# Joint image-text attention block on one core: image V in 512-column tiles with a shared 128-column remainder, and text scores, image gate rows and text V moved behind all image scores

## The chip, the cores and the metric

The kernel runs on one core of a Trainium2 chip, in one launch. The metric is device time in microseconds, the median of several executions. The core has a matrix engine (TensorE, PE in the profile), a vector engine (VectorE, DVE), a scalar engine (ScalarE, ACT), a general engine (GpSimd, POOL) and a queue engine that only issues transfers (SyncE, SP). Each engine works through its own instruction list in order; they meet at semaphores.

## The reference

Two batches. Each has 256 image tokens and 32 text tokens of width D = 1152; everything is bfloat16. Fourteen matrices of 1152 x 1152 (2.65 MB each) are read, each once.

```python
mod_i = silu(c) @ wmod_img          # first three of six slices used: shift, scale, gate
mod_t = silu(c) @ wmod_txt
hi = layernorm(x_img) * (1 + sci) + shi
ht = layernorm(x_txt) * (1 + sct) + sht
qi, ki, vi = split(hi @ wqkv_img);  qt, kt, vt = split(ht @ wqkv_txt)
q, k, v = concat([qt, qi]), concat([kt, ki]), concat([vt, vi])
p = softmax(q @ k.T * D ** -0.5)
at, ai = split(p @ v)
out_i = x_img + gai * (ai @ wo_img)
out_t = x_txt + gat * (at @ wo_txt)
```

## The kernel before

A D of 1152 is nine blocks of 128 (`KT`), so every product over D is a run of nine matrix instructions that add up in one PSUM tile. PSUM has eight tiles in two pools: six of `ps_mm` and two of `ps_tr`; a tile is taken in turn, and a new user waits until the reader of the old one is done.

**Loads.** SP issues all weight loads into five slots of one matrix each, in a fixed order: `x_i` for batch 0 (L103), the image scale `w_sc_i` in four pieces (L107), then image V `w_v_i` in five pieces (L109) with the two tiles of `x_i` of batch 1 between them (L112), then image shift, image Q, text shift, text x, image K, text scale, text Q, text K, image gate, text V, the two output matrices and the text gate. A load waits for the last use of its slot's former content; the last piece of `w_v_i` has four of the nine blocks.

**Image stage** (to the first Q instruction). LayerNorm: image tiles 0 and 2 get their sums on ACT (`ln_sums`, L199 and L200), tiles 1 and 3 theirs on DVE (`ln_stats`, L192); ACT works out the reciprocal deviations (L209, L210), DVE normalises (L214) into `xn`. PE transposes `xn` (`x_transposes`, six 128x128 transposes to a PSUM tile `tp`, copied to `xT_i` by ACT or DVE at L250). The scale rows come from `sc_rows`, matrix instructions that use 32 columns of the array (four side by side), and DVE turns them to columns (`sc_cols`, L257) and multiplies `xT_i` into `hS_i` (`x_scale`, L264). V needs only the scaled input; what the shift adds to V is a row that is added later. `v_open` runs image V in accumulators of 384 columns: six (`V0`) for batch 0 over eight of the nine blocks, then the transposes of batch 1, the ninth block, then the six of batch 1 (`V1`), with the shift rows `mod_rows_of(w_sh_i)` between. The layer norm of batch 1 stands in the ACT and DVE lists behind the scaling of batch 0:

```python
sc_cols(5, KT)
x_scale(4, KT, 0)
s2 = ln_sums(x_i[:, 2, :], xn_b[1][:, 0, :])
...
v_open(V0, 0, K8)
out01, out31 = x_transposes(0, 1), x_transposes(3, 1)
```

Then `hT_i`, with the shift, is made in place of `xT_i` (L346, L349), and `shift_v_rows` works out the row that V lacks.

**Q and K** (`qk_img`, 81 instructions of 512 columns each, then `qk_txt`) run without a gap on PE; DVE sums the text shift beside them (`shift_part`, L427).

**Attention.** Scores are nine instructions for each of four image query tiles (`scores_img`) and one text tile (`scores_txt`, 32 columns of the array). `soft_max`, `soft_exp` and `soft_div` are the DVE maximum (L556), the ACT exponential (L563), and the division on DVE (L568, L570), in which POOL writes a second copy of the last 32 columns (L571). `img_gate` runs the image gate rows on PE (32 columns), ACT copies them out (L508), and POOL writes them to a scratch tensor with two DMAs (L510), from which `img_gate_spread` later reads them back for all partitions (L521). `p_transposes` turns the probabilities for the second product, and ACT copies them (L606); `v_txt` is text V, 64 columns of the array, two side by side. The order on PE is: two image scores, text scores, gate rows, two image scores, nine transposes, text V, nine transposes, then `attn_pair`, then `out_img` and `out_txt`. `keep_in_program_order` (`pin`) holds all PE instructions, and the marked ones of the other engines, in the order of the source.

Of the kernel before, what the change touches and what calls it, by code (L numbers as in the profile page):

```python
# [14 lines left out]
def kernel(  # L15
# [14 lines left out]
    nc = tc.nc  # L30
    bf = mybir.dt.bfloat16
    f32 = mybir.dt.float32
# [27 lines left out]
    def mm(*a, **k):  # L60
        return pin(nc.tensor.matmul(*a, **k))  # L61

    def tr(*a, **k):
        return pin(nc.tensor.transpose(*a, **k))  # L64
# [38 lines left out]
    nc.sync.dma_start(x_i[:, 0:TPB, :], x_img[0].rearrange("(p t) d -> p t d", t=TPB))  # L103
# [4 lines left out]
    for r0, r1 in ((0, 1), (1, 2), (2, 3), (3, 5), (5, KT)):  # L108
        nc.sync.dma_start(w_v_i[:, r0:r1, :], v_v[:, r0:r1, :])  # L109
        if r0 in (1, 3):  # L110
            i = TPB + r0 // 2
            nc.sync.dma_start(x_i[:, i, :], x_img[1].rearrange("(p t) d -> t p d", t=TPB)[i - TPB])  # L112
# [67 lines left out]
    def evac(out_ap, in_ap):  # L180
        if evac_idx[0] % 2 == 0:
            nc.vector.tensor_copy(out_ap, in_ap)
        else:
            nc.scalar.copy(out_ap, in_ap)
        evac_idx[0] += 1
# [21 lines left out]
    def ln_rstd(var, np_, sign=1.0):  # L207
        rstd = small.tile([P, 1], f32, tag="rstd")
        pin(nc.scalar.activation(rstd[0:np_, :], var, ACT.Ln, bias=eps_t[0:np_], scale=sign))  # L209
        pin(nc.scalar.activation(rstd[0:np_, :], rstd[0:np_, :], ACT.Exp, scale=-0.5))  # L210
        return rstd

    def ln_norm(x_ap, mean, rstd, np_, out_ap):
        pin(nc.vector.tensor_scalar(out_ap, x_ap, mean, rstd[0:np_, :], op0=ALU.subtract, op1=ALU.mult))  # L214

    xn_b = [act.tile([P, TPB, D], bf, tag="A%d" % b, name="xn%d" % b) for b in range(B)]
# [13 lines left out]
    sc_ps = ps_tr.tile([P, KT, LW], f32, tag="tr")  # L230
# [11 lines left out]
    def x_transposes(k0, b):  # L242
        tp = (ps_tr if b else ps_mm).tile([P, 3, NI], bf, tag="tr" if b else "mm", name="tp")
        for kt in range(k0, k0 + 3):
            for t in range(TPB):
                tr(tp[:, kt - k0, t * P:(t + 1) * P], xn_b[b][:, t, kt * P:(kt + 1) * P], ident[:])
        dst = xT_i[:, k0:k0 + 3, b * NI:(b + 1) * NI]

        def copy_out():
            pin(nc.vector.tensor_copy(dst, tp[:]) if k0 == 3 else nc.scalar.copy(dst, tp[:]))  # L250

        return copy_out
# [14 lines left out]
    v_b = [act.tile([P, TPB, D], bf, tag="A%d" % b, name="v%d" % b) for b in range(B)]  # L267
    accs = {}

    def v_open(ids, k0, k1, engines=None):  # L270
        for key in ids:
            if key not in accs:
                accs[key] = ps_mm.tile([P, CH], f32, tag="mm", name="vps")
        for kt, (i, cc) in [(kt, key) for kt in range(k0, k1) for key in ids]:
            mm(accs[(i, cc)][:], lhsT=hS_i[:, kt, i * P:(i + 1) * P], rhs=w_v_i[:, kt, cc * CH:(cc + 1) * CH],
               start=(kt == 0), stop=(kt == KT - 1), skip_group_check=True)
            if kt == KT - 1:
                dst = v_b[i // TPB][:, i % TPB, cc * CH:(cc + 1) * CH]
                if engines:
                    pin((nc.scalar.copy if engines[ids.index((i, cc))] == "A" else nc.vector.tensor_copy)(  # L280
                        dst, accs[(i, cc)][:]))
                else:
                    evac(dst, accs[(i, cc)][:])

    V0, V1 = [[(i, cc) for i in range(b * TPB, (b + 1) * TPB) for cc in range(NCH)] for b in range(B)]

    def ln_norm_dve(i, mv):
        ln_norm(x_i[:, i, :], mv[:, 0:1], ln_rstd(mv[:, 1:2], P), P, xn_b[i // TPB][:, i % TPB, :])

    def ln_norm_act(i, sm):  # L290
        ln_norm(x_i[:, i, :], sm[:, 0:1], ln_rstd(sm[:, 2:3], P, sign=-1.0), P, xn_b[i // TPB][:, i % TPB, :])

    s0 = ln_sums(x_i[:, 0, :], xn_b[0][:, 0, :])
# [3 lines left out]
    ln_norm_act(0, s0)  # L297
    for out in [x_transposes(k0, 0) for k0 in (0, 3, 6)]:
        out()
    sc_rows(0, 4)  # L300
    sc_rows(4, 7)
    warm_up(1)
    sc_rows(7, K8)
    warm_up(1)
    sc_rows(K8, KT)
    sc_cols(0, 1)
    x_scale(0, 1, 0, step=1)
    sc_cols(1, 5)
    x_scale(1, 4, 0)
    sc_cols(5, KT)  # L310
    x_scale(4, KT, 0)
    s2 = ln_sums(x_i[:, 2, :], xn_b[1][:, 0, :])
    ln_var(s2)
    m3 = ln_stats(x_i[:, 3, :], P)
    r2, r3 = ln_rstd(s2[:, 2:3], P, sign=-1.0), ln_rstd(m3[:, 1:2], P)
    ln_norm(x_i[:, 2, :], s2[:, 0:1], r2, P, xn_b[1][:, 0, :])
    ln_norm(x_i[:, 3, :], m3[:, 0:1], r3, P, xn_b[1][:, 1, :])
    v_open(V0, 0, K8)
    out01, out31 = x_transposes(0, 1), x_transposes(3, 1)
    out01()  # L320
    out31()
    x_scale(0, 6, 1)
    v_open(V0[0:2], K8, KT, engines="AA")
    x_transposes(6, 1)()
    v_open(V0[2:], K8, KT, engines="VAVA")
    x_scale(6, KT, 1)
    v_open(V1[0:2], 0, KT)
# [9 lines left out]
    v_open(V1[2:3], 0, KT)  # L337
# [12 lines left out]
    for key in V1[3:]:  # L350
        v_open([key], 0, KT)
# [130 lines left out]
    def v_txt(r):  # L482
        ps = ps_mm.tile([P, VC], f32, tag="mm")
        for kt in range(KT):
            for g in range(2):
                c0 = g * HD + r * VC
                mm(ps[64 * g:64 * g + NTT, :], lhsT=hT_t[:, kt, :], rhs=w_v_t[:, kt, c0:c0 + VC],
                   start=(kt == 0), stop=(kt == KT - 1), tile_position=(0, 64 * g))
        return ps
# [11 lines left out]
    def mod_rows(w_blk, si):  # L501
        gps = ps_mm.tile([P, VC], f32, tag="mm")
        for kt in range(KT):
            for g in range(NGG):
                mm(gps[32 * g:32 * g + 32, :], lhsT=sT32[:, kt, :], rhs=w_blk[:, kt, g * VC:(g + 1) * VC],
                   start=(kt == 0), stop=(kt == KT - 1), tile_position=(0, 32 * g))
        g_sb = work.tile([P, VC], bf, tag="garow")
        pin(nc.scalar.copy(g_sb[:], gps[:]))  # L508
        for b in range(B):
            nc.gpsimd.dma_start(gsc[si, b, :].rearrange("(g j) -> g j", g=NGG), g_sb[b:P:32, :])  # L510
# [5 lines left out]
    def img_gate():  # L516
        mod_rows(w_ga_i, 0)
# [8 lines left out]
    def txt_gate():  # L526
        mod_rows(w_ga_t, 1)
        for g in range(2):
            for b in range(B):
                r0 = 64 * g + 32 * b  # L530
                nc.gpsimd.dma_start(gbf[r0:r0 + NT, :, :],
                                    gsc[1, b, :].rearrange("(r g j) -> g r j", r=2, g=2)[g].partition_broadcast(NT))

    shift_v_rows()
# [59 lines left out]
    def p_transposes(b):  # L594
        pT = work.tile([P, 3, NTOK], bf, tag="pT")
        tiles = [(range(3), ps_tr)] if b == 0 else [((2,), ps_mm), (range(2), ps_tr)]
        for kjs, pool in tiles:
            pT_ps = pool.tile([P, 8 * P], bf, tag="tr" if pool is ps_tr else "mm", name="pT_ps")
            txt = [(2, pbs["t"], ident2 if b else ident)]
            img = [(qi, pbs[(b, qi)], ident) for qi in range(TPB)]  # L600
            for n, kj in enumerate(kjs):
                for qi, pb, perm in (txt + img if b else img + txt):
                    o = n * NTOK + qpos[b][qi]
                    k0 = kj * P - (NT * b if kj == 2 else 0)
                    tr(pT_ps[:, o:o + P], pb[:, k0:k0 + P], perm[:])
            pin(nc.scalar.copy(pT[:, kjs[0]:kjs[-1] + 1, :],  # L606
                               pT_ps[:, 0:len(kjs) * NTOK].rearrange("p (k n) -> p k n", n=NTOK)))
        pTs[b] = pT

    def attn_keys(tiles, first):  # L610
        for b, dt in tiles:
            for kj in range(2):
                mm(tiles[(b, dt)][:], lhsT=v_b[b][:, kj, dt * P:(dt + 1) * P], rhs=pTs[b][:, kj, :],
                   start=(first and kj == 0), stop=(not first and kj == 1))
# [25 lines left out]
    sp = {key: scores_img(*key) for key in I[:2]}  # L640
# [5 lines left out]
    st = scores_txt()  # L646
    half = work.tile([NTT, NTOK], f32, tag="half", bufs=1)
    pin(nc.scalar.copy(half[:], st[NTT:P, :]))
    soft_div(I[1])
    img_gate()  # L650
    pin(nc.vector.tensor_add(half[:], st[0:NTT, :], half[:]))
    soft_max("t", half, NTT)
    soft_exp("t")
    for key in I[2:]:
        sp[key] = scores_img(*key)
    soft_max(I[2], sp[I[2]], P)
    soft_exp(I[2])
    soft_div("t")
    soft_max(I[3], sp[I[3]], P)
    soft_exp(I[3])  # L660
    soft_div(I[2])
    soft_div(I[3])
    p_transposes(0)
    for r in range(2):
        v_txt_out(r, v_txt(r))
    p_transposes(1)
# [76 lines left out]
```

## Time and profile before

| What | us |
|---|---|
| median of three executions (120.5, 121.08, 120.5) | 120.5 |
| the profiled execution: time / span of its trace | 120.5 / 118.6 |
| PE busy | 110.5 (93%) |
| DVE busy / ACT busy / POOL busy | 71.1 / 46.1 / 12.3 |
| mean DMA rate over the span | 346 GB/s |
| first image V instruction | 12.67 |
| first image Q instruction | 37.04 |
| first score instruction | 78.52 |
| first `attn_pair` instruction | 88.29 |
| last PE instruction group starts / span ends | 114.91 / 118.6 |

The span reaches from the first to the last instruction in the trace; the time has 1.9 us more around it. The granted TensorE clock is 0.999 over the span. In a profile line, `out<-in` are tile names, `x18` the number of instructions in a group, and a bracket the idle time of the engine just before, with what ended it.

### The profile page before, as it was taken

The numbers are of one execution on the slowest core, as the hardware profiler recorded it, in microseconds if no ns is written. First come the engines' busy times: TensorE is split into PE (matmuls) and PEld (weight loads), VectorE is DVE, ScalarE is ACT, GpSimd is POOL, SyncE is SP. The second block draws the span as 40 slices with busy tenths as digits, with TensorE's granted clock in tenths as the row PEclk, the third lists the DMA queues.
The fourth block names the chain that finished last, engine by engine and source line by source line (L and its number), as shares of the span: only waits on it lengthen the run. The fifth ranks groups of instructions, "written<-read, shape, count | busy, mean of one in ns | idle before, by whom it ended". The sixth has DMA issues, their size and how long they took to land.

```text
span 118.6 us, 2503 instructions
## 1 busy us (share of the span) xinstructions
PE 110.5 (93%) x1035; PEld 64.7 (55%) x1035; DVE 71.1 (60%) x151; ACT 46.1 (39%) x96; POOL 12.3 (10%) x34
## 2 busy tenths in 40 slices
PE   5999791999999999999999999999999999999990
PEld 1346450655655444444445448687876656566660
DVE  3561863084593999999999030016756656346571
ACT  4765451091292358952521233326557700100000
POOL 7300000000000000000000000002617000470000
PEclk9999999999999999999999999999999999999999
DMA  4999999999999999999999999999999999224223
GB/s 124 368 393 401 409 407 408 413 411 411 410 404 386 319 405 410 416 402 413 390 375 412 412 412 413 405 410 406 411 404 411 417 379 363 100 73 83 100 50 100
DMA packets 19045, 41.02 MB, mean 346 GB/s; under 512 B 1195, under 2 KB 1851, under 8 KB 19035
## 3 DMA queue, kind: packets, MB, share of 16 engines
q1 hardware_dynamic: 18160, 39.86, 87.4%
q0 software_dynamic: 480, 0.89, 2.6%
q10 hardware_dynamic: 395, 0.12, 0.4%
q8 instruction: 8, 0.13, 0.4%
q14 instruction: 2, 0.02, 0.0%
HBM read 39.52 MB, written 1.34 MB: 345 GB/s over the span
## 4 chain that ended last, share of the span: by engine, by line
PE 79%; DMA 15%; SPq 1%; DVE 1%; ACT 1%; issue 0%
PE ps L61 52%; PE vps L61 11%; DMA t<-in_wqkv_img_dram 8%; DMA t<-in_wmod_img_dram 7%; PE gps L61 5%; PE aps L61 5%; PE sps L61 4%; PE pT_ps L64 1%; SPq L107 1%; PE tp L64 1%; ACT xT_i L250 1%; DVE tmp L684 1%; DVE o L685 0%; SPq L103 0%; PE tpt L64 0%
## 5 line engine op out<-in xcount | busy, mean ns | idle before, releaser
L61 PE MATMUL ps<-xT_i,t 128*128 128x512 bf16 x162 | 35.7, 379 | 0.0
L61 PEld LDWEIGHTS <-t 128*128 128x128 bf16 x324 | 20.5, 98 | 18.9 <-issue 0.5
L427 DVE SCALAR_TENSOR_TENSOR acc_sh<-t,sTf,acc_sh 128x1152 f32<-128x1152 bf16 x16 | 21.4, 1408 | 0.0
L61 PE MATMUL vps<-t,hS_i 128*128 128x384 bf16 x108 | 18.4, 326 | 3.2 <-DMA t<-in_wqkv_img_dram 2.6
L61 PE MATMUL ps<-t,aT 128*128 128x384 bf16 (+3 forms) x153 | 20.3, 308 | 0.0
L61 PEld LDWEIGHTS <-aT 128*128 128x128 bf16 (+1 forms) x153 | 12.9, 101 | 7.2 <-issue 0.8
L61 PEld LDWEIGHTS <-hS_i 128*128 128x128 bf16 x108 | 10.3, 98 | 10.3 <-issue 3.0
L357 ACT CAST qkT<-ps 128x512 bf16<-128x512 f32 (+2 forms) x11 | 6.1, 551 | 14.8 <-PE ps L61 13.5
L684 DVE TENSOR_TENSOR tmp<-ps,gb 128x384 bf16<-128x384 f32 (+2 forms) x13 | 6.8, 526 | 8.0 <-PE ps L61 8.0
L571 POOL TENSOR_SCALAR pb<-e,rs 128x32 bf16<-128x32 f32 (+1 forms) x5 | 2.1, 413 | 76.9 <-DVE rs L568 76.9
L355 ACT ACTIVATE qkT<-ps 128x512 bf16<-128x512 f32 (+2 forms) x11 | 6.1, 561 | 8.7 <-PE ps L61 8.7
L61 PE MATMUL wps<-warm 128*128 128x512 bf16 x24 | 7.9, 479 | 1.5 <-DVE unit L129 1.5
L556 DVE TENSOR_REDUCE nmx<-sps 128x1 f32<-128x288 f32 x4 | 1.8, 458 | 9.7 <-PE sps L61 9.7
L61 PEld LDWEIGHTS <-sT 128*32 128x32 bf16 x180 | 4.6, 96 | 2.1 <-issue 1.5
L250 ACT COPY xT_i<-tp 128x768 bf16<-128x768 bf16 x4 | 3.1, 808 | 6.5 <-PE tp L64 6.5
L61 PE MATMUL sps<-qkT 128*128 128x288 bf16 (+1 forms) x54 | 5.5, 287 | 0.0
L620 DVE TENSOR_SCALAR aT<-aps,svc 128x288 bf16<-128x288 f32 x9 | 4.1, 512 | 2.2 <-PE aps L61 2.2
L61 PEld LDWEIGHTS <-warm 128*128 128x128 bf16 x24 | 2.6, 115 | 5.2 <-issue 2.4
L61 PE MATMUL gps<-t,sT 128*32 128x288 bf16 x144 | 5.2, 287 | 0.0
L61 PE MATMUL aps<-pT,v 128*128 128x288 bf16 x36 | 5.1, 287 | 0.0
L61 PE MATMUL ps<-hT_t,t 128*128 128x64 bf16 x162 | 5.1, 193 | 0.0
L622 ACT ACTIVATE aT<-aps,svc 128x288 bf16<-128x288 f32 x9 | 4.3, 500 | 1.4 <-PE aps L61 1.4
(112 smaller groups left out, 104.3 us busy)
## 6 DMA issues: line engine op xcount, KB each, us to landing
t<-in_wqkv_txt_dram SPq DMA_DIRECT2D x3, 2592.0 KB, 16.4
t<-in_wmod_img_dram SPq DMA_DIRECT2D x2, 2592.0 KB
t<-in_wmod_txt_dram SPq DMA_DIRECT2D x2, 2592.0 KB, 16.6
t<-in_wqkv_img_dram SPq DMA_DIRECT2D x3, 864.0 KB, 14.3
t<-in_wqkv_img_dram SPq DMA_DIRECT2D x1, 2592.0 KB
t<-in_wo_img_dram SPq DMA_DIRECT2D x3, 864.0 KB, 8.1
t<-in_wmod_txt_dram SPq DMA_DIRECT2D x2, 864.0 KB, 13.1
t<-in_wo_txt_dram SPq DMA_DIRECT2D x1, 1440.0 KB
```

The lines of the kernel that those rows point to most:

```text
L61: return pin(nc.tensor.matmul(*a, **k))
L64: return pin(nc.tensor.transpose(*a, **k))
L107: nc.sync.dma_start(w_sc_i[:, r0:r1, :], sc_v[:, r0:r1, :])
L250: pin(nc.vector.tensor_copy(dst, tp[:]) if k0 == 3 else nc.scalar.copy(dst, tp[:]))
L355: nc.scalar.mul(out_ap, in_ap, SCALE)
L357: nc.scalar.copy(out_ap, in_ap)
L427: pin(nc.vector.scalar_tensor_tensor(acc, w_sh_t[:, kt, :], col, acc, op0=ALU.mult, op1=ALU.add))
L556: pin(nc.vector.reduce_max(nmx[0:qn, :], sps[0:qn, :], axis=AX.X, negate=True))
L571: pin(nc.gpsimd.tensor_scalar(pb[0:qn, NI + 2 * NT:NI + 3 * NT], e[0:qn, NI:NTOK], rs[0:qn, :], 0.0, op0=ALU.mult, op1=ALU.add))
L620: nc.vector.tensor_scalar(dst, tiles[(b, dt)][:], bias, None, op0=ALU.add)
L622: nc.scalar.activation(dst, tiles[(b, dt)][:], ACT.Identity, bias=bias)
L684: nc.vector.tensor_mul(tmp[:, 0:n], ps[:, 0:n], gb[:, b, c0:c0 + n])
```

## The change

In the image stage it loads all of `x_i` first, and cuts `w_v_i` into six pieces, the last two of two blocks each. It moves the layer norm of batch 1 ahead of the scale rows, and its transposes between them. V runs in tiles of 512 columns: `A0` are four for batch 0, `A1` the first of each tile of batch 1; the second of those follow, and then `v_last`, one PSUM tile with the last 128 columns of all four image tiles. In the attention it puts text scores, gate rows and the first half of text V behind the four image scores; text V runs in 32 columns of the array, four side by side (72 instructions for 36). The copy of the gate rows (`gate_row`) and their two DMAs come after the exponential of the text scores and before `soft_div("t")`. The 18 transposes of the probabilities are adjacent, in four groups, two of which DVE copies.

```diff
-    nc.sync.dma_start(x_i[:, 0:TPB, :], x_img[0]...)
+    for b in range(B):
+        nc.sync.dma_start(x_i[:, b * TPB:(b + 1) * TPB, :], x_img[b]...)
...
-    for r0, r1 in ((0, 1), (1, 2), (2, 3), (3, 5), (5, KT)):
+    for r0, r1 in ((0, 1), (1, 2), (2, 3), (3, 5), (5, 7), (7, KT)):
         nc.sync.dma_start(w_v_i[:, r0:r1, :], v_v[:, r0:r1, :])
-        if r0 in (1, 3):
-            ...
...
+    VW = 512
+    A0 = [(0, 0), (0, 1), (1, 0), (1, 1)]
+    A1 = [(2, 0), (3, 0)]
...
     ln_norm_act(0, s0)
+    s2 = ln_sums(x_i[:, 2, :], xn_i[:, 2, :])
+    m3 = ln_stats(x_i[:, 3, :], P)
+    ln_var(s2)
+    r3, r2 = ln_rstd(m3[:, 1:2], P), ln_rstd(s2[:, 2:3], P, sign=-1.0)
+    ln_norm(x_i[:, 3, :], m3[:, 0:1], r3, P, xn_i[:, 3, :])
+    ln_norm(x_i[:, 2, :], s2[:, 0:1], r2, P, xn_i[:, 2, :])
     for out in [x_transposes(k0, 0) for k0 in (0, 3, 6)]:
         out()
     sc_rows(0, 4)
+    warm_up(3)
     sc_rows(4, 7)
-    warm_up(1)
+    out01 = x_transposes(0, 1)
+    out31 = x_transposes(3, 1)
     sc_rows(7, K8)
-    warm_up(1)
     sc_rows(K8, KT)
+    out61 = x_transposes(6, 1)
+    out01()
     sc_cols(0, 1)
     x_scale(0, 1, 0, step=1)
     sc_cols(1, 5)
-    ...
+    x_scale(1, 3, 0)
+    v_open(A0, 0, 3)
+    out31()
+    out61()
+    x_scale(0, 3, 1)
     sc_cols(5, KT)
-    ...
+    for k0 in (3, 6):
+        for b in range(B):
+            x_scale(k0, k0 + 3, b)
+    v_open(A1, 0, 3)
+    v_open(A0 + A1, 3, KT - 2)
+    v_open(A0 + A1, KT - 2, KT, kt_major=False)
...
+    v_open([(2, 1)], 0, KT)
     p_sh = mod_rows_of(w_sh_i, sT32)
...
+    v_open([(3, 1)], 0, KT)
+    def v_last():
+        vps = ps_mm.tile([P, NIT, P], f32, tag="mm")
+        for i in range(NIT):
+            for kt in range(KT):
+                mm(vps[:, i, :], lhsT=hS_i[:, kt, i * P:(i + 1) * P], rhs=w_v_i[:, kt, 2 * VW:D], ...)
+        evac(v_i[:, :, 2 * VW:D], vps[:])
...
             for g in range(2):
-                mm(ps[64 * g:64 * g + NTT, :], lhsT=hT_t[:, kt, :], ..., tile_position=(0, 64 * g))
+                for b in range(B):
+                    c0, r0 = g * HD + r * VC, 64 * g + NT * b
+                    mm(ps[r0:r0 + NT, :], lhsT=hT_t[:, kt, NT * b:NT * b + NT], ..., tile_position=(0, r0))
...
-    sp = {key: scores_img(*key) for key in I[:2]}
+    sp = {key: scores_img(*key) for key in I}
+    st = scores_txt()
+    img_gate()
+    vt = [v_txt(0)]
...
     soft_exp("t")
...
+    gate_row()
     soft_div("t")
...
+    v_txt_out(0, vt[0])
+    vt.append(v_txt(1))
+    p_transposes(0, (0, 1), ps_tr, nc.scalar.copy)
+    v_txt_out(1, vt[1])
+    p_transposes(0, (2,), ps_mm, nc.vector.tensor_copy)
+    p_transposes(1, (2,), ps_mm, nc.vector.tensor_copy)
+    p_transposes(1, (0, 1), ps_tr, nc.scalar.copy)
```

## The prediction

> **What bounds the kernel now.** First the chain that ended last, since PE is busy 93% of the span and shares alone do not say where a microsecond is worth anything. Columns: start, length, what.
>
> ```profile
> 10.48 9.75 DMA t<-in_wqkv_img_dram
> 20.23 0.04 issue
> 20.27 3.09 PE vps L61 x18
> ...
> 35.82 1.22 PE gps L61 x36
> 37.04 19.53 PE ps L61 x90
> ...
> 78.52 2.92 PE sps L61 x36
> 81.44 1.10 PE gps L61 x36
> 82.55 2.31 PE sps L61 x18
> 84.86 0.50 PE pT_ps L64 x9
> 85.36 2.33 PE ps L61 x36
> 87.69 0.61 PE pT_ps L64 x9
> 88.29 5.78 PE aps L61 x54
> ```
>
> The reader sees a transfer up to 20.23, then PE alone, without a hole, to 114.91. So from the first Q instruction (37.04) on, only fewer PE cycles or a new hole can move the end; before 20.23 it is the arrival of `w_v_i`. The timeline of PE shows the hole, that of ACT what batch 1 waits for:
>
> ```profile
> 12.67 5.05 PE L61 MATMUL vps<-t,hS_i 128*128 128x384 bf16 x30 [0.69 <-DVE hS_i L264]
> 20.27 3.09 PE L61 MATMUL vps<-t,hS_i 128*128 128x384 bf16 x18 [2.56 <-DMA t<-in_wqkv_img_dram]
> ```
>
> ```profile
> 13.37 1.17 ACT L199 ACTIVATE xn<-x_i 128x1152 bf16<-128x1152 bf16 x1 [2.74 <-DMA x_i<-in_x_img_dram]
> ```
>
> Image V begins at 12.67, uses five blocks of weights, and starves for 2.56 us until the one piece with the last four has landed. It has nothing else to do, because batch 1 is not normalised and transposed yet: its `x_i` comes at 13.37, behind other loads.
>
> **Front, step 1: when V can start.** Loads come in issue order at the page's rate, 0.36 to 0.41 MB per us. Running totals from the rate row: 1.18 MB (all of `x_i`) at 5.2 us, with `w_sc_i` 3.83 MB at 11.9, with `w_v_i` 6.49 MB at 18.4. In before, the issue that waits for the last piece of `w_sc_i` ran at 11.19, where the total (3.24 MB) is at 10.4: a piece is usable 0.75 us behind its total. So `x_i` of batch 1 is there at 5.9 and the last scale piece at 12.6 (before: 11.2). ACT is free at 7.8. The two sums of tile 2 take 2.55 us (in before 13.37 to 15.92): 10.35. Variance, two reciprocal deviations and two norms at the spacings of before (L209 to L214) end at 11.9. ACT then copies two of the three `xT_i` tiles of batch 0, which now stand behind these sums, 0.8 us each: 11.15 to 12.65; DVE copies the third, to 12.4. PE's first two transpose groups of batch 1 wait for those two buffers and for norm 2: 12.0 to 12.45 and 12.5 to 12.9. Behind them in PE's list stand the last scale rows, 12.9 to 13.4. From the end of scale rows to V took 0.64 us in before (12.03 to 12.67). **V starts at 14.05, 1.38 us later**; `out61`'s transposes (13.4 to 13.8, after a copy on ACT) fit before that.
>
> **Front, step 2: what V then takes.** The 81 Q instructions of 512 columns with nine others took 19.53 us: 217 ns each. 72 of them: 15.62 us. `v_last` has 36 of 128 columns; the nearest row is the 128x128 transposes, same shape of both operands, 9 in 0.50 us, 55.6 ns: 2.00 us. Two row runs at 1.22: 2.44. In all 20.06 us, if PE never waits. DVE: it scales 128x256 in about 0.22 us; by its list block 0 is ready at 14.05, block 2 at 14.9, batch 1's first three at 16.05, block 3 at 17.05 and 17.7, all at 19; PE wants them at 14.05, 15.8, 16.6, 17.9, 23.1. Weights: blocks 5 and 6 at about 18.5 against 20.5, the last two by 20.2 against 23.1; the hole closes. `w_sh_i`: total at 24.9, plus at most 1.7, against 27.7. `w_q_i`: its last piece is shown by the SP timeline, where the load that waits for it goes out:
>
> ```profile
> 33.06 0.37 SPq L89 DMA_DIRECT2D t<-in_wqkv_img_dram  x1
> ```
>
> **Q starts at 14.05 + 20.06 = 34.11 instead of 37.04: 2.93 us earlier**, 1.05 us after its weights. Where the gain comes from, as a cross-check: 2.56 (hole) + 0.23 (wait for a transpose copy, L250) + about 1.3 (18 transposes taken out of the V run) + 0.3 (columns in fewer instructions), less 1.38.
>
> The Trainium skill, "TensorE: Matmul & The Clock Gate", section Back-to-back issue gap, gives about 81 ns for each 128-column matmul in a stream with its weight load, and that speaks against `v_last`. By it the 36 would take 2.9 us and the whole sum be 0.9 us worse, an estimate from that page; the row says 55.6 ns, and I take the row.
>
> **Middle.** Nothing is edited, so the 2.93 us stay if no load is late. Totals at the page's rate plus 1.7 us (what `w_q_i`'s 33.06 stands behind its total, 31.34), against the moment of need 2.93 us earlier: image K 47.3 against 51.7; text Q 60.3 against 68.7; text K 67.4 against 73; image gate 73.9 against 80.7; text V 80.4 against 81.9; image output 86.9 against 91.6; text gate 93.4 against 97.5. The slack of Q and text V, 1 and 1.5 us, is what the range must hold. DVE's shift sum waits 4.44 us for PE at its end (L447), so it is no bound.
>
> **Tail, PE cycles.** With 0 the first score instruction: four image scores at 1.10, end 4.41; text 0.75 (2.92 less 2.2), 5.16; gate 1.13, 6.29; text V 72 instructions, priced by the gate's 36 in 1.10 as 30.6 ns: 2.20 (before 36 in 2.33), 8.5; 18 transposes about 1.05. That would be 9.55 for 9.77, through fewer changes of array shape.
>
> **Tail, the new wait.** The transposes of key block 2 need the last-32-column copy that POOL writes for text, and POOL's list now has the two scratch DMAs ahead of it. In before POOL did this:
>
> ```profile
> 83.30 1.33 POOL L510 DMA_DIRECT2D mod_scratch<-g_sb  x2 [0.70 <-ACT g_sb L508]
> 84.67 0.30 POOL L571 TENSOR_SCALAR pb<-e,rs 64x32 bf16<-64x32 f32 x1
> ```
>
> There they followed a gate copy at 82.60, one ACT step ahead of the text exponential. Now, with the durations of these rows: `half` on ACT 5.2 to 5.6, image exponential 3 to 6.1, add and maximum on DVE 5.65 to 6.6, text exponential 6.7 to 7.35, gate copy 7.25 to 7.65, POOL's two DMAs 7.95 to 9.28, its copy 9.32 to 9.62. PE arrives after six transposes and two image ones at 9.0, waits to 9.68, then ten transposes: **attention at 10.24 instead of 9.77, 0.47 us later**. Everything on PE stands behind that wait. The ACT and DVE copies of the groups end at 9.7, 10.2 and 10.9, each before its reader. The gate spread begins about 2.5 us later (POOL's wait for the scratch write), lands at about 20 against the first output tile at 17.5; DVE waits, but PE has six buffers, each 1.46 us, and DVE needs 0.92 per chunk, so that is caught up and costs nothing.
>
> The Trainium skill, "SBUF — State Buffer", section Who interferes with whom, says that while VectorE holds the port it shares with GpSimd, GpSimd cannot write the descriptors of its DMAs (about 620 ns alone, 3100 beside such a copy). Two issues at that would add about 5 us to the wait, an estimate from that page, and undo the gain. The row shows 1.33 us for two beside DVE work at 82.84 to 84.35; I take the row.
>
> **Sum.** 120.5 - 2.93 + 0.47 = **118.0 us**, made against the profiled execution, whose time equals the median, 120.5. What can be told from no change is about 0.5%, 0.6 us.
>
> **Rivals.**
> - *Loads take back part (0.20).* Q's or text V's last piece comes 1 to 1.5 us later than reckoned, or V starts later by as much since a step of the ACT chain slips. For it: slacks of 1.05 and 1.5 us, loads at the rate limit throughout. Against: the bytes ahead of both are the same as before. Time 119.0.
> - *No wait in the tail (0.09).* POOL's DMAs start earlier than 7.95 or take no 1.33 us, and attention begins at 9.55: 120.5 - 2.93 - 0.2 = 117.4.
> - *Slower: `x_i` of batch 1 lands late (0.08).* Its ACT sums now stand ahead of batch 0's copies and its transposes ahead of the last scale rows, so if it lands not at 5.9 but with the second scale piece at 11.2, everything up to V moves 3.4 us (11.2 for 7.8): V at 17.45, time 118.0 + 3.4 = 121.4. It decides from a landing at 10.3 (no change). For it: `x_i` of tile 2 came at 13.37 although issued at 4.46. Against: that was behind 3.8 MB of loads; here only 0.59 MB is ahead.
> - *Nothing to be seen (0.08).* V at 16.5 by a slip of half that size, or DMA issues on POOL at twice their price (1.3) together with 1 us lost to loads: 119.9 to 121.1.
>
> **How the numbers follow.** The main case, 0.55, is 118.0. Faster by over 0.5%: 0.55 + 0.20 + 0.09 = 0.84; same 0.08; slower 0.08. The range starts at the case without a tail wait and V 0.2 us early (117.2), and ends at the loads case with 0.5 more, or `v_last` at 81 ns on top of 0.6 lost (119.5).
>
> **What would show it.** Right: first V instruction near 14, no wait of `vps` for a DMA, Q at about 34.1, scores at about 75.6, and a wait of PE for POOL's `pb` before attention at about 85.8. Wrong: a DMA wait at the first Q or text V instruction; V not before 15.5; transposes of batch 1 held by ACT past 13; or an attention that begins under 9.6 us behind the first score.

## The result, and the profile after

The changed kernel takes 118.8 us, the median of six executions (118.58 to 119.04), against a forecast of 118.0 with a range of 117.2 to 119.5. Its ratio to the kernel before is 0.9853, with a 95% interval of 0.9821 to 0.9884; the means behind it are 118.81 and 120.59 us, a fall of 1.8 us. The span of the profiled execution fell as much, from 118.6 to 116.8 us. The ratios here and below leave out executions that took over 1.5% longer than the fastest of their kernel, and with them most, not all, of those in which the granted TensorE clock fell; what that fall is comes with the experiment that fills the hole.

The chain that ended last (start, length, what) no longer has the transfer of image V in it. From 14.36 it is PE up to the text scores:

```profile
14.36 13.77 PE vps L61 x63
28.13 1.22 PE gps L61 x36
29.35 4.06 PE vps L61 x45
33.41 1.22 PE gps L61 x36
34.62 19.53 PE ps L61 x90
...
76.29 5.15 PE sps L61 x54
```

The first Q instruction is at 34.62 (37.04 before), the first score at 76.29 (78.52). In the timeline of PE the hole in V is gone, and there is a short wait for the second scale piece instead:

```profile
11.92 0.55 PE L61 MATMUL sc_ps<-t,sT 128*32 128x288 bf16 x12 [0.39 <-DMA t<-in_wmod_img_dram]
...
14.36 13.77 PE L61 MATMUL vps<-t,hS_i 128*128 128x512 bf16 x63
```

The timeline of ACT shows the sums of batch 1's first tile starting right behind batch 0's work, without the 2.74 us wait for its load that stood there before:

```profile
8.03 1.15 ACT L197 ACTIVATE xn_i<-x_i 128x1152 bf16<-128x1152 bf16 x1
```

The load that waits for `w_q_i` goes out when it did before, so Q now starts 1.5 us behind its weights instead of 4.0 (timeline of SP):

```profile
33.11 0.37 SPq L89 DMA_DIRECT2D t<-in_wqkv_img_dram  x1
```

Then comes the new wait. The chain leaves PE behind the text scores, goes through their softmax, the gate copy on ACT and the two DMA issues on POOL, and comes back to PE at the transposes:

```profile
83.54 0.29 ACT g_sb L520
83.83 0.29 issue
84.12 0.73 POOL mod_scratch L522
84.84 0.00 issue
84.85 0.60 POOL mod_scratch L522
85.44 0.04 issue
85.48 0.31 POOL pb L587
85.79 0.04 issue
85.83 0.73 PE pT_ps L64 x10
86.57 5.78 PE aps L61 x54
```

Attention begins 86.57 - 76.29 = 10.28 us behind the first score, 0.51 us more than the 9.77 of before. From there on nothing moved: from the start of attention to the last `out_img` group it is 26.61 us, against 26.62.

### The profile page after: what moved, and what is told of

It is laid out like the page before. It is cut to its first block, busy times and chain, and to the rows that moved or that the text cites. A ratio compares the mean times of both kernels' runs of the same rounds, so it can differ in the third digit from the quotient of the medians.

```text
span 116.8 us, 2569 instructions
## 1 busy us (share of the span) xinstructions
PE 110.6 (95%) x1072; PEld 63.3 (54%) x1072; DVE 72.3 (62%) x153; ACT 44.1 (38%) x92; POOL 12.3 (11%) x34
## 4 chain that ended last, share of the span: by engine, by line
PE 82%; DMA 8%; DVE 2%; POOL 1%; ACT 1%; SPq 1%; issue 1%; DVEq 0%
PE ps L61 51%; PE vps L61 15%; DMA t<-in_wmod_img_dram 8%; PE aps L61 5%; PE sps L61 4%; PE gps L61 4%; POOL mod_scratch L522 1%; PE sc_ps L61 1%; SPq L104 1%; PE tp L64 1%; PE pT_ps L64 1%; DVE tmp L701 1%; ACT e L579 1%; DVE o L702 0%; DVE half L671 0%
## 5 line engine op out<-in xcount | busy, mean ns | idle before, releaser
L61 PE MATMUL vps<-t,hS_i 128*128 128x512 bf16 (+1 forms) x108 | 17.9, 326 | 0.1
L61 PEld LDWEIGHTS <-hS_i 128*128 128x128 bf16 x108 | 9.0, 98 | 8.7 <-DVE hS_i L264 0.4
L180 DVE CAST v_i<-vps 128x512 bf16<-128x512 f32 x5 | 3.5, 692 | 7.5 <-PE vps L61 7.5
L182 ACT CAST v_i<-vps 128x512 bf16<-128x512 f32 x4 | 2.3, 580 | 9.9 <-PE vps L61 9.9
L61 PE MATMUL aps<-pT,v_i 128*128 128x288 bf16 x36 | 5.1, 287 | 0.0
```

## The experiments

**The image stage alone.** The tail is put back as it was, on the changed image stage.

```diff
-    sp = {key: scores_img(*key) for key in I}
-    st = scores_txt()
-    img_gate()
-    vt = [v_txt(0)]
+    sp = {key: scores_img(*key) for key in I[:2]}
     ...
```

> The changed image stage with the old order of scores, gate, text V and transposes. Theory (all gain is in front, the tail costs about 0.5 us through the wait for GpSimd): first score instruction at about 76.3 as in the changed kernel, 9.77 us from there to attention as in the kernel before, time about 0.5 us below the changed kernel, 118.2 to 118.3. Rival (the tail's fewer changes of array shape are a part of the gain): 0.2 us or more above the changed kernel.

It took 118.55 us, ratio 0.9834 (0.9814 to 0.9854), with spans of 116.1 to 116.4 against 116.6 to 116.8 of the changed kernel. In the chain the first score is at 76.32 and attention at 86.09, which is the 9.77 us of before. The gain is all in front, and the tail gives a part of it back: by the trace 0.51 us, by the spans some 0.45, by the medians, which were not taken side by side, only 0.25.

**The tail alone.** The old image stage with the new tail, that is, the attention part of the change put into the kernel before.

> The old image stage with the new order of scores, gate, text V and transposes. Theory: first score instruction at 78.5 as before, attention 10.25 us behind it with a PE wait of about 0.6 us for GpSimd's copy, time 0.5 us above the kernel before. Rival (fewer changes of array shape win): 0.2 us below the kernel before.

The ratio is 1.0063 (1.0015 to 1.0111), slower. Two of the executions in it had a clock of 0.986; the six of its twelve in which the clock held take 121.10 us on average, against 120.69 for those of the kernel before, 0.4 us more. In its chain the first score stands at 80.86 and attention at 91.14: 10.28 us again, with a PE wait of 0.56 us for POOL. The rival, that fewer changes of array shape win, falls. The profile is of an execution in which the clock fell, and its first score is 2.3 us later than in the kernel before, for a reason told where the hole is filled.

**The gate row late.** Only the order of two lines.

```diff
-    gate_row()
     soft_div("t")
+    gate_row()
```

> The changed kernel with the gate row's copy and its two GpSimd DMAs behind the division of the text scores, so that GpSimd's copy of the last columns comes first. Theory: no wait of PE for GpSimd, attention 9.7 us behind the first score instead of 10.28, time 0.55 us below the changed kernel; the gate spread comes later by about 0.4 us and costs nothing. Rival (the transposes are held by something just behind that wait, the text exponential or the ACT copies): less than 0.2 us gained.

Measured: 118.39 us, ratio 0.9832 (0.9803 to 0.986), and 118.38 beside 118.87 for the changed kernel when both were run together a second time (below). PE waits for POOL no more. What is late next is a short wait for ACT's first copy, in the chain:

```profile
84.75 0.45 PE pT_ps L64 x6
85.20 0.02 issue
85.22 0.65 ACT pT L621
85.87 0.04 issue
85.92 5.94 PE aps L61 x54
```

The chain gives an instruction that waited its own start (85.92 here), and one that did not wait the end of the work before it (86.57 for attention in the changed kernel), so the two can't be set against each other. The timeline of PE gives the own starts of both, first in the changed kernel, then here:

```profile
76.12 5.29 PE L61 MATMUL sps<-qkT 128*128 128x288 bf16 x54
...
86.40 0.90 PE L61 MATMUL aps<-pT,v_i 128*128 128x288 bf16 x6
```

```profile
76.15 5.29 PE L61 MATMUL sps<-qkT 128*128 128x288 bf16 x54
...
85.92 0.90 PE L61 MATMUL aps<-pT,v_i 128*128 128x288 bf16 x6
```

Attention begins 10.28 us behind the first score in the changed kernel and 9.77 us here, as in the kernel before (88.13 - 78.35 = 9.78). So two DMA issues of 1.33 us, moved ahead of a copy of 0.3 us that PE needs, cost the changed kernel 0.51 us, and the times of the two kernels run together differ by as much, 0.49. The 0.2 us that the new order was to save on PE do not show yet, because of the wait for ACT.

**The cut of the last V load, alone, in the kernel before.**

```diff
-    for r0, r1 in ((0, 1), (1, 2), (2, 3), (3, 5), (5, KT)):
+    for r0, r1 in ((0, 1), (1, 2), (2, 3), (3, 5), (5, 7), (7, KT)):
```

> The kernel before with one edit: the last piece of image V (four blocks) is cut into two of two blocks. Theory (the hole at 17.7 to 20.27 is there because the layer norm of batch 1 is late and PE has nothing else): blocks 5 and 6 land near 18.5, PE waits 0.8 us there and then works on; the hole falls from 2.56 to about 1.0 and the time by 1.5 us. Rival (pieces in flight share the rate, so the first half comes hardly earlier): blocks 5 and 6 near 19.8, gain 0.5 us or less. A gain of 1.5 us would mean that over half of the front's gain needs neither the 512-column tiles nor the early layer norm.

119.59 us, ratio 0.993 (0.9908 to 0.9951). The timeline of PE gives the hole:

```profile
18.79 3.09 PE L61 MATMUL vps<-t,hS_i 128*128 128x384 bf16 x18 [1.09 <-DMA t<-in_wqkv_img_dram]
```

It fell from 2.56 to 1.09 us; blocks 5 and 6 are there at 18.75, and the first score comes at 77.20 instead of 78.52. So 1.3 of the 2.2 us in front can be had with one edit of a tuple, without 512-column tiles and without the early layer norm. The time fell by less: 0.8 us by the ratio, 1.0 by the spans (117.7 to 118.0, against a mean of 118.8 for the kernel before). In the profile the other 0.4 us went at the very end, where the waits for the output transfers took 1.5 us in all instead of 1.1; the reason stays open.

**The same load uncut, in the changed kernel.**

```diff
-    for r0, r1 in ((0, 1), (1, 2), (2, 3), (3, 5), (5, 7), (7, KT)):
+    for r0, r1 in ((0, 1), (1, 2), (2, 3), (3, 5), (5, KT)):
```

> The changed kernel with image V's last four blocks in one load again, as before. Theory (in the changed kernel PE has enough other work: it wants block 5 at about 20.9 and the whole piece is there by 20.3): no hole, time within 0.3 us of the changed kernel, so the cut of that load is worth 1 us only where the layer norm of batch 1 is late. Rival (the cut is what the gain is made of): a hole of 1 us or more at block 5 and a time 1 us above the changed kernel.

118.82 us, ratio 0.9822 (0.9779 to 0.9865), and no `vps` wait for a DMA. Here the cut is worth nothing: a smaller last piece shortens the hole, more work ready for PE closes it, and the two gains do not add up.

**Text V in 64 columns, in its new place.**

```diff
-                for b in range(B):
-                    c0, r0 = g * HD + r * VC, 64 * g + NT * b
-                    mm(ps[r0:r0 + NT, :], lhsT=hT_t[:, kt, NT * b:NT * b + NT], ..., tile_position=(0, r0))
+                c0 = g * HD + r * VC
+                mm(ps[64 * g:64 * g + NTT, :], lhsT=hT_t[:, kt, :], ..., tile_position=(0, 64 * g))
```

> The changed kernel with text V in 64 columns of the array, two side by side (36 instructions), as before, in its new place. Theory: 2.33 us for text V instead of 2.21 and two changes of array shape more; PE then waits that much less for GpSimd, so the time to attention stays at 10.28 us and the time within 0.2 us of the changed kernel. Rival (32 columns save PE time that reaches the end): 0.2 us or more above.

118.81 us, ratio 0.9821 (0.9779 to 0.9863). In the chain attention begins 86.02 - 75.74 = 10.28 us behind the first score, the same to the hundredth. The wait for POOL shrank from 0.56 to 0.44 us, by just what the slower text V took: while PE ends in a wait, PE cycles saved ahead of it are worth nothing.

**Batch 1's input late.** Its load moves behind the second scale piece: the prediction's slower rival.

```diff
-    for b in range(B):
-        nc.sync.dma_start(x_i[:, b * TPB:(b + 1) * TPB, :], ...)
+    nc.sync.dma_start(x_i[:, 0:TPB, :], ...)
...
         nc.sync.dma_start(w_sc_i[:, r0:r1, :], sc_v[:, r0:r1, :])
+        if r0 == 4:
+            nc.sync.dma_start(x_i[:, TPB:NIT, :], ...)
```

> The changed kernel with the load of batch 1's input moved behind the second scale piece: the prediction's slower case made on purpose. Theory (the ACT sums of tile 2 set when V starts): the load lands at about 11.2, the sums start there instead of at 8.0, the scale rows and V move by 3.2 us, V starts at 17.6, the time is about 3 us above the changed kernel, 121.7 to 122. Rival (what sets V's start in the changed kernel is the landing of the scale pieces, which here come earlier): V at 14.4 to 15 and the time within 0.6 us of the changed kernel.

123.43 us, ratio 1.0206 (1.0157 to 1.0254). ACT starts the sums at 11.24, and the timeline of PE shows what follows:

```profile
15.37 0.96 PE L64 MATMUL tp<-ident,xn_i 128*128 128x128 bf16 x12 [3.22 <-ACT xT_i L251]
...
17.37 15.34 PE L61 MATMUL vps<-t,hS_i 128*128 128x512 bf16 x63
```

V starts at 17.37, near the 17.45 of the prediction: with the load late, the ACT chain sets it. But the time is 1.6 us more than this explains. The 63 V instructions take 15.34 us where the changed kernel needs 13.77, behind a PE wait of 3.22 us. In the stages view (stretch, length, busy time by engine, then granted clock, DMA share, GB/s) the mean clock is 0.57 there:

```profile
17.00:21.00 4.00, 3.89 (x15) 1.48 (x13) 3.90 (x19) 0.80 (x1) 0.00 (x0) 0.57 1.04 407
21.00:26.00 5.00, 5.00 (x25) 2.25 (x23) 0.82 (x5) 0.00 (x0) 0.00 (x0) 1.00 1.04 412
```

**The hole filled with dummy work, in the kernel before.** The tail-alone profile had shown the same thing, in the hole that the kernel before has. Its stages:

```profile
17.88:20.85 2.97, 0.00 (x1) 0.00 (x0) 1.31 (x4) 0.50 (x2) 0.00 (x0) 1.00 1.04 406
20.85:25.60 4.75, 4.75 (x21) 2.50 (x21) 0.00 (x0) 0.00 (x0) 0.00 (x0) 0.64 1.04 412
```

Behind 2.97 us without PE work, 18 matrix instructions took 4.76 us that take 3.09 in the profile of before, behind 2.56 us. Eight matrix instructions on constants, into a PSUM tile that nobody reads, fill the hole:

```diff
-    v_open(V0, 0, K8)
+    v_open(V0, 0, 5)
+    fill = ps_tr.tile([P, 512], f32, tag="tr", name="fill")
+    for _ in range(8):
+        mm(fill[:], lhsT=warm[:, 0:P], rhs=warm[:], start=True, stop=True)
+    v_open(V0, 5, K8)
```

> The kernel before with eight matrix instructions on constants put into the hole of image V (1.74 us of its 2.56). Nothing of the result depends on them. In the profile of the kernel with the old image stage and the new tail the hole was 2.97 us and the granted clock in the 4.75 us behind it 0.64; in the profile before, 2.56 us and 1.00. Theory (a hole of near 3 us is what takes the clock down): granted clock 0.99 or more over the span of every execution, time at the lowest of the kernel before, about 120.5. Rival (the clock falls for another reason): executions with a span clock of 0.98 to 0.99 remain, as the kernel before has them.

The time is 120.62 us, ratio 0.9982 (0.9957 to 1.0008): no gain where the clock holds. In the timeline of PE only 0.33 us of hole are left:

```profile
18.18 1.89 PE L61 MATMUL fill<-warm 128*128 128x512 bf16 x8
20.41 3.09 PE L61 MATMUL vps<-t,hS_i 128*128 128x384 bf16 x18 [0.33 <-DMA t<-in_wqkv_img_dram]
```

The clock is what it changes. All 12 executions had a mean granted clock of 0.995 or more over the span and took 120.32 to 120.75 us. Of the kernel before, run beside these experiments 47 times (17 of them beside this one), 25 executions (6 of those 17) had a clock of 0.981 to 0.986 and took 121.93 to 123.22 us, the other 22 took 120.24 to 121.43. The fall is due to the hole: dummy work in it, which speeds up nothing else, takes it away.

**A better tail.** The late gate row, and VectorE copies the first group of transposes ahead of the second half of text V, ScalarE the three others. The changed kernel and the late-gate kernel ran beside it on the same chip.

```diff
+    soft_div("t")
     gate_row()
-    soft_div("t")
     v_txt_out(0, vt[0])
     vt.append(v_txt(1))
-    p_transposes(0, (0, 1), ps_tr, nc.scalar.copy)
+    p_transposes(0, (0, 1), ps_tr, nc.vector.tensor_copy)
     v_txt_out(1, vt[1])
-    p_transposes(0, (2,), ps_mm, nc.vector.tensor_copy)
-    p_transposes(1, (2,), ps_mm, nc.vector.tensor_copy)
+    p_transposes(0, (2,), ps_mm, nc.scalar.copy)
+    p_transposes(1, (2,), ps_mm, nc.scalar.copy)
```

> The changed kernel with the gate row behind the text division (as in the kernel with the late gate row), and with VectorE copying the first group of transposes ahead of the second half of text V, ScalarE the other three groups. Theory: the 0.16 us that PE still waited for ScalarE's first copy (85.75 to 85.92 in the late-gate kernel) go, attention 9.5 us behind the first score, time 0.7 us below the changed kernel of the same call. Rival: the second half of text V or ScalarE's copies come late for their readers and give it back, so nothing on top of the late gate row's 0.4 us.

> The late-gate kernel, once more beside the changed one. Theory: 0.4 to 0.6 us below the changed kernel of the same call. Rival: the 0.4 us between the first two measurements lay between the chips' calls, less than 0.2 us.

> The changed kernel itself, once more, so that the two versions below stand beside it on one chip. Both theories: 118.8 us, attention 10.28 us behind the first score.

Measured together: 118.06 us (ratio 0.9772, 0.9718 to 0.9825), 118.38 for the late gate row (0.9799, 0.9737 to 0.9861), 118.87 for the changed kernel (0.9838, 0.9777 to 0.99). The intervals of the ratios overlap; the traces tell the versions apart. In the chain of the best, PE runs through from the scores to the end of attention:

```profile
76.27 5.13 PE sps L61 x54
81.40 1.10 PE gps L61 x36
82.50 2.21 PE ps L61 x72
84.71 1.11 PE pT_ps L64 x18
85.82 5.81 PE aps L61 x54
```

Attention comes 9.55 us behind the first score, 0.22 below the kernel before and 0.73 below the changed one, whose chains have no wait just ahead of attention either; the medians of the changed kernel and this one differ by 0.8. Against the late-gate kernel it is 0.19 us by the own starts in the timeline (85.69 - 76.11 = 9.58 for 9.77). This version beats both kernels.

## Why the prediction was right or wrong

The direction, the two mechanisms and the range held; the size of the gain was forecast too large, 2.5 us for the 1.8 that the means (120.59 and 118.81) and the spans (118.6 and 116.8) show.

- *When V can start* was the term with the largest error: 14.05 forecast, 14.36 in the profile, and 14.2 to 14.5 in all but one of the eight profiles with this image stage (13.71 there). The step that failed is "a piece is usable 0.75 us behind its total". It held where it was read, but the load that waits for the last scale piece goes out at 13.35 in the changed kernel, 1.45 us behind the total of 11.9. The second piece, whose total is 3.24 MB and so at 10.4, is there at 11.87, as late; in six of the eight profiles PE waits 0.4 to 0.9 us for it, and the chain of the changed kernel runs through this wait. The transposes of batch 1 and V stand behind it and go later. In the one profile with V at 13.71 PE did not wait for that piece, but ACT's sums also began 0.5 us earlier there, so it does not part the two.
- *What V takes* was 20.26 us for 20.06. The 512-column instructions come at 219 ns for 217, and the 36 of 128 columns at (4.06 - 9 x 0.217) / 36 = 59 ns for 55.6. The Trainium skill's 81 ns ("TensorE: Matmul & The Clock Gate", section Back-to-back issue gap) is not what this stream shows. No wait came in.
- *The cross-check* counts the 2.56 us of the hole as one gain and does not say which edit brings it. With the early layer norm and the uncut piece there is no wait; with the cut alone 1.09 us of it are left, and 1.3 us of the gain in front are there. The terms of 1.3 us for the transposes and 0.3 us for the wider tiles were not tried singly.
- *The middle* took 41.67 us for 41.48. The eleven other profiles have 41.46 to 41.69, so this is scatter, and the kernel before stood near its lower end; the chain shows gaps of 0.03 to 0.05 us called "issue" in some profiles and none in others. Their cause was not tried. No load was late; the slack that the rival of late loads needed was there.
- *The tail* was forecast to 0.04 us: 10.24 for 10.28, with the wait for POOL that was named, behind two DMA issues of 1.33 us. The place and the cause are right; that the sum is so close is luck in part, since PE went on at 9.54 for 9.68, and the ten transposes behind the wait took 0.73 us for 0.56. The DMA issues took 1.33 us beside VectorE work, as the row had said. The multiple of it that the Trainium skill, "SBUF — State Buffer", gives for a copy on VectorE (its figures stand in the section A bandwidth-pool intuition that's wrong) was not put to the test: VectorE ran additions there, at 84.04 to 85.24, and reductions beside the row of before. The gate spread was late as reckoned (VectorE waits 3.29 us for it at the first output tile, until 96.19) and cost nothing.
- *Around the span* the changed kernel's profiled execution has 2.2 us and that of before 1.9; the sum had kept 1.9. It is not scatter alone: the kernel before has 1.9 on average over 47 executions and so have the three other kernels with its image stage, while the nine runs with the changed image stage average 2.0 to 2.2 each. Where these 0.1 to 0.3 us go stays open.
- *The slower rival* had its place and point right and its price too low: 121.4 against 123.43. V came 3.0 us later than in the changed kernel, for 3.4 reckoned, and the sum left out that the clock falls behind a PE wait of 3.2 us, which costs 1.6 us more. In the rival *Nothing to be seen*, half of the 3.4 us would put V at 15.75, not at 16.5.

Together: 0.31 + 0.20 + 0.19 + 0.04, less 0.1 at the end, are the 0.6 us between the span's forecast fall of 2.46 and the measured one of 1.8 (the 0.1 is the stretch from the last PE group to the end of the span, 3.6 us for 3.7).

## What to carry to other kernels

Where PE starves for a load, ask first how large the piece is that it waits for, and only then what else PE could do; here the first took over half of the hole, the second all of it, and the gains did not add. A DMA issue on GpSimd took 0.60 to 0.73 us of that engine's list here: put it behind the small copies that the critical engine waits for, not ahead. PE cycles saved in front of a wait of PE are worth nothing until the wait is gone. And when two kernels are compared by the start of a group, take both starts from the same view and in the same way, with or without a wait ahead.

## What the runs showed of the hardware

A PE hole of about 3 us can be followed by half the granted clock, in some executions and not in others. Read in stages of 0.1 us, the clock in both traces is still 1.00 when PE starts again. It falls to 0.50 only later, 0.8 us behind the hole of 2.97 us and 1.8 us behind the one of 3.22 us, and stays there for 3.4 us in both; the 0.64 and 0.57 above are means over longer stretches. All six executions of the kernel with the hole of 3.22 us had a span clock of 0.986; behind the 2.56 us of the profile before the clock stayed at 1.00; with 1.09 us none of six executions showed the fall. It costs 1.6 to 1.7 us in the two traces. The Trainium skill, "TensorE: Matmul & The Clock Gate", Part 1, says that the clock falls back after an idle window of about 3.4 us, and that the window runs freely. A hole of 2.97 us is shorter than that figure; that the fall begins at no fixed distance from the hole, and comes in some executions only, fits a window that is not tied to the hole. What starts it, no run here shows by itself. The kernel before loses this time in about half of its executions, and the changed kernel, with no hole, in none of the twelve seen. Most of that benefit is not in the ratios above.
